# Moving eight short query-weight loads from ahead of the first key load to behind it, in a streaming decode kernel

## Chip, cores and metric

The kernel runs on one core of one Trainium2 chip. The metric is device microseconds of one execution; the time given for a kernel is the median of its runs. A difference of 0.2% (0.8 us here) is about what a measurement of this kernel can tell from no change.

## What is computed

Two branches share one input row `x` (1 x 1024) and are mixed by a gate:

```python
g = sigmoid((x * gate_w).sum(-1, keepdims=True))
# A: attention of one query row over a cache of 65536 positions, 32 query heads on 4 key/value heads of 128
q = (x @ wq).reshape(1, 1, 32, 128).transpose(0, 2, 1, 3)      # wq 1024 x 4096
scores = einsum('bhqd,bhkd->bhqk', q, repeat(k_cache, 8)) * 128 ** -0.5
a = (softmax(scores) @ repeat(v_cache, 8)).transpose(...).reshape(1, 1, 4096) @ wo   # wo 4096 x 1024
# B: gated MLP with a spatial weight of size 1 x 1
z = gelu(x @ w_in)                                             # w_in 1024 x 3584
b = (z[..., :1792] * (layernorm(z[..., 1792:]) * w_sp + b_sp)) @ w_out
out = g * a + (1 - g) * b
```

All inputs are bf16. The keys and the values are 67.1 MB each, `wq` and `wo` 8.4 MB each, `w_in` 7.3 MB, `w_out` 3.7 MB: 162 MB are read for an output of 2 KB.

## The kernel before

**A stream of large loads.** `stream` is a list of loads in a fixed order (lines 347 to 363): `wq`, the first 8 MB of keys (`load_k2(0, 0)`, called the first keys below), `w_in`, 4 MB of keys, 4 MB of keys, `w_out`, then keys and values in turns of 8 MB, at last `wo` in five parts. All are issued on SyncE's DMA queue (SP) by `issue()` at line 392, in the order of the list, into a ring in the on-chip memory with five places of 4 MB. The two keys loads of the first 8 MB take places 0 and 1, `wq` and `w_in` both take the region `VB` (places 3 and 4).

**What holds a load back.** A load may be recorded once its place's earlier user is done (`done(key)` calls `issue()` again), and then its DMA waits on SP for the engine that read the place last. So `w_in` waits for the last TensorE matmul that reads `wq` (line 507), and everything later in the list stands behind it on SP, since SP takes its instructions in order.

**The cut of `wq`.** Of the `wq` load the last 512 columns of each partition's row are left off (`w -= MC`, line 391). These 128 rows of 1 KB are fetched by `few_rows()` (line 409) with eight short DMAs, four of 20 rows into 5 x 4 pieces and four of 12 rows into 3 x 4 pieces; they land in place 2. `few_rows()` is called right behind the `wq` load, so SP's order is: `wq`, eight short loads, first keys, `w_in`, and so on.

**The query projection.** One recorded operation on TensorE (lines 494 to 511) holds 63 matmuls on the main part of `wq` (helper lines 261 and 263) and then eight on the short rows (line 507). The recorder (`Recorder.emit`) puts all of an operation's waits ahead of its first instruction, so the 63 matmuls too wait for the eight short loads. Behind it VectorE copies the result (L513), TensorE transposes it (L517), and after two more small steps (L520 to L528) GpSimd writes the padded query (`q_piece`, L536). All key work stands behind this: VectorE transposes a quarter of a keys block at a time (`k_piece`, L548, 128 x 2048 as f32), TensorE multiplies it with the query (L261, L263).

**Ahead of the start.** `R.ahead` says how many of SP's first DMAs are put ahead of the barrier with which the engines start together: 10 before, which are `wq`, the eight short loads and the first keys. `R.early` does the same for four tiny loads on ScalarE's queue.

Of the kernel before, what the change touches and what calls it, by code (L numbers as in the profile page):

```python
# [138 lines left out]
def bass_gated_mix__gqa_block_cached__mixer_gmlp__decode_kernel(  # L139
# [115 lines left out]
    R = Recorder()  # L255
# [50 lines left out]
    MC, MB = 512, 8  # L306
# [68 lines left out]
    def grains(off, w):  # L375
        return list(range(off // GRAN, (off + w + GRAN - 1) // GRAN))

    def issue():

        while issued[0] < len(stream):  # L380
            n = issued[0]
            keys, off, src = stream[n]
            w = src.shape[1]
            gr = grains(off, w)
            if any(k not in used for x in gr if x in owner for k in owner[x]):
                return
            for j, x in enumerate(gr):
                owner[x] = (keys[j * len(keys) // len(gr)],)
            cut = keys == [("wq", 0)]
            if cut:  # L390
                w -= MC
            P("SP", lambda e, o=OFF["RING"] + off, w=w, src=src[:, :w]: e.dma_start(arena[:, o:o + w], src),
              w=[("slot", x) for x in gr], dma="s%d" % gr[0])
            if cut:
                few_rows()
            issued[0] += 1

    def few_rows():

        ps = arena[:, 0:1].ap[0][0]  # L400
        at, gr, r0 = OFF["RING"] + M_AT, grains(M_AT, MC * MB), 0
        for ne, nj, j0 in FEW:
            for lo in range(4):
                a = arena[:, at:at + 1]
                a = bass.AP(tensor=a.tensor, offset=a.offset + lo * ps + MC * j0, ap=[[4 * ps, ne], [MC, nj], [1, MC]])
                b = A_wq[0:1, :]
                b = bass.AP(tensor=b.tensor, offset=b.offset + WQ_N * (KC * (r0 + nj * lo) + KC - 1) + WQ_N - MC,
                            ap=[[WQ_N * KC * 4 * nj, ne], [WQ_N * KC, nj], [1, MC]])
                P("SP", lambda e, a=a, b=b: e.dma_start(a, b), w=[("few", lo + j0)] + ([] if lo + j0 else [("slot", x) for x in gr]),  # L409
                  dma="few%d" % (lo + j0))  # L410
            r0 += 4 * ne * nj
        owner.update({x: (("wq", 0),) for x in gr})
# [6 lines left out]
    def done(key):  # L419
        used.add(key)  # L420
        issue()

    issue()


# [401 lines left out]
    P("DVE", lambda e: e.tensor_copy(orow[0:W0 + NW, :], fb[0:W0 + NW, 0:QW]), w=["orow", "fb"])  # L827
    store()

    R.ahead = 2 + MB  # L830
    R.early = 4
    R.emit(nc)

# [27 lines left out]
```

## Time and profile before

| | |
|---|---|
| time, median of 3 runs | 380.53 us (380.39 to 380.82) |
| the profiled execution: its own time, its span | 380.59 us, 379.3 us |
| bytes read from HBM | 162.01 MB, 427 GB/s over the span |
| TensorE, VectorE busy | 61%, 54% of the span |
| mean granted TensorE clock | 0.838 |
| SP issue of one short load | 0.70 to 0.93 us, 8 of them |

The span goes from the first to the last instruction of the profiled execution; 1.3 us of its time lie outside. In the profile SPq is SP's queue of DMA issues, PE is TensorE, DVE VectorE, POOL GpSimd, ACT ScalarE; L392 is line 392 of the kernel. A row of the timeline gives the start in us, the duration in us, engine, line, operation, output and input, the count, and in brackets the idle time before it and what ended it.

### The profile page before, as it was taken

The page shows a single profiled execution, that of the slowest core. Times are in us where ns is not written, and L with a number is a line of the kernel's source. Part 1 is how long each engine was busy: PE and PEld are TensorE (multiplying, and loading weights), DVE is VectorE, ACT ScalarE, POOL GpSimd, SP SyncE. Part 2 cuts the span into 40 slices and gives each one's busy share as a digit, 9 for nine tenths or more (in the row PEclk, how much of TensorE's full clock was granted, in tenths as well). Part 3 has the DMA queues.
Part 4 walks back from the last instruction along what each step waited for, and adds up shares of the span by engine and source line. Part 5 has one row for each costly group of instructions (what it writes and reads, how often), then busy time and mean ns, then how long its engine had stood idle before and what let it go on. Part 6 is the DMA issues. An engine that isn't in the chain of part 4 may idle for free.

```text
span 379.3 us, 2599 instructions
## 1 busy us (share of the span) xinstructions
PE 229.9 (61%) x1452; PEld 57.9 (15%) x844; DVE 205.6 (54%) x168; ACT 23.3 (6%) x24; POOL 9.3 (2%) x36
## 2 busy tenths in 40 slices
PE   0062289566648934895389328951995189737296
PEld 0011011011201200121012001220111011201024
DVE  1411487778479625965496249745873387412020
ACT  1000000010420000002200000022000000220000
POOL 1400000000000000000000000000000000000000
PEclk9997589798959985998599959995899589958599
DMA  9999999999999999999999999999999999999896
GB/s 436 435 415 408 433 419 422 442 456 438 408 435 442 435 444 422 422 442 435 442 437 442 429 422 429 444 442 435 429 408 430 442 435 442 437 442 435 384 432 273
DMA packets 3822, 162.17 MB, mean 428 GB/s; under 512 B 484, under 2 KB 612, under 8 KB 868
## 3 DMA queue, kind: packets, MB, share of 16 engines
q1 hardware_dynamic: 3776, 162.01, 98.9%
q8 instruction: 9, 0.15, 0.1%
q10 hardware_dynamic: 36, 0.00, 0.0%
q14 instruction: 1, 0.01, 0.0%
HBM read 162.01 MB, written 0.00 MB: 427 GB/s over the span
## 4 chain that ended last, share of the span: by engine, by line
DMA 61%; PE 17%; DVE 17%; SPq 2%; ACT 1%; issue 1%
DMA arena<-in_A_k_cache_dram 46%; DVE arena L548 16%; DMA arena<-in_A_wo_dram 8%; DMA arena<-in_A_v_cache_dram 7%; PE scp L261 7%; PE scp L263 6%; SPq L409 2%; PE obt L261 2%; PE obt L263 1%; DVE arena L585 1%; PE fbt L766 1%; ACT arena L580 1%; DVE arena L670 0%; DVE arena L668 0%; PE fbt L714 0%
## 5 line engine op out<-in xcount | busy, mean ns | idle before, releaser
L548 DVE STREAM_TRANSPOSE arena<-arena 128x2048 f32<-128x2048 f32 x64 | 143.0, 2284 | 54.9 <-DMA arena<-in_A_k_cache_dram 40.1
L261 PE MATMUL scp<-arena 128*128 128x512 bf16 (+1 forms) x274 | 111.6, 424 | 94.4 <-DVE arena L548 93.9
L263 PE MATMUL scp<-arena 128*128 128x512 bf16 (+1 forms) x275 | 110.2, 418 | 0.0
L261 PE MATMUL obt<-arena 128*64 128x512 bf16 (+2 forms) x334 | 60.7, 404 | 15.1 <-DMA arena<-in_A_v_cache_dram 14.9
L263 PE MATMUL obt<-arena 128*64 128x512 bf16 (+2 forms) x333 | 60.1, 400 | 0.0
L261 PEld LDWEIGHTS scp<-arena 128*128 128x128 bf16 (+1 forms) x274 | 27.5, 104 | 205.1 <-issue 103.9
L585 DVE STREAM_TRANSPOSE arena<-arena 128x2048 bf16<-128x2048 bf16 x7 | 16.2, 2311 | 27.0 <-PE obt L263 24.8
L580 ACT ACTIVATE arena<-arena 128x2048 bf16<-128x2048 f32 x8 | 16.0, 2002 | 217.2 <-DVE arena L577 194.1
L261 PEld LDWEIGHTS obt<-arena 128*64 128x64 bf16 (+1 forms) x334 | 17.7, 109 | 65.3 <-issue 58.5
L565 DVE TENSOR_SCALAR_CACHE_REDUCE arena<-scp 128x2048 f32<-128x2048 f32 x8 | 18.3, 2292 | 16.0 <-PE scp L263 16.0
L614 DVE RECIPROCAL arena<-mbt 128x1 f32<-128x1 f32 x4 | 0.6, 138 | 17.5 <-PE mbt L609 17.5
L588 DVE STREAM_TRANSPOSE arena<-arena 128x1024 bf16<-128x1024 bf16 x2 | 2.5, 1245 | 12.9 <-PE obt L263 12.9
L536 POOL COPY arena<-arena 32x32 bf16<-32x32 bf16 x16 | 3.3, 204 | 227.4 <-PE scp L263 207.7
L467 PE MATMUL scp<-arena 8*128 8x1 bf16 x8 | 0.7, 198 | 13.0 <-DVE arena L462 13.0
L627 PE MATMUL mbt<-arena 128*64 128x128 bf16 x8 | 1.3, 314 | 7.7 <-DVE arena L621 7.7
L766 PE MATMUL fbt<-arena 128*32 128x128 bf16 x128 | 4.2, 220 | 1.2 <-DMA arena<-in_A_wo_dram 1.2
L280 DVE MEMSET mbt<- 128x512 f32 x1 | 0.5, 485 | 7.7 <-PEq L846 7.7
L513 DVE CAST arena<-obt 97x1024 bf16<-97x1024 f32 x1 | 1.2, 1224 | 6.2 <-PE obt L507 6.2
L475 PE MATMUL mbt<-arena 1*128 1x2 bf16 x1 | 0.2, 158 | 7.2 <-DMA arena<-in_B_b_sp_dram 7.2
L827 DVE CAST arena<-fbt 36x128 bf16<-36x128 f32 x1 | 0.3, 283 | 7.3 <-PE fbt L766 7.3
L477 DVE COPY arena<-mbt 128x2 f32<-128x2 f32 x1 | 0.2, 158 | 7.3 <-PE mbt L475 7.3
L577 DVE TENSOR_REDUCE arena<-mbt 128x1 f32<-128x32 f32 x4 | 0.8, 192 | 6.0 <-PE mbt L574 6.0
(99 smaller groups left out, 62.5 us busy)
## 6 DMA issues: line engine op xcount, KB each, us to landing
arena<-in_A_k_cache_dram SPq DMA_DIRECT2D x2, 4096.0 KB, 31.7
arena<-in_A_wq_dram SPq DMA_DIRECT2D x1, 8064.0 KB, 21.7
arena<-in_B_w_in_dram SPq DMA_DIRECT2D x1, 7168.0 KB, 28.9
arena<-in_A_wo_dram SPq DMA_DIRECT2D x1, 4096.0 KB, 38.5
arena<-in_B_w_out_dram SPq DMA_DIRECT2D x1, 3584.0 KB, 20.2
arena<-in_A_wo_dram SPq DMA_DIRECT2D x1, 2048.0 KB, 27.6
arena<-in_A_wo_dram SPq DMA_DIRECT2D x1, 1280.0 KB, 30.3
arena<-in_A_wo_dram SPq DMA_DIRECT2D x1, 512.0 KB, 31.0
```

Source lines behind the costliest of these rows:

```text
L261: return e.matmul(*a, **kw)
L263: one = e.matmul(*a, **kw).ins
L409: P("SP", lambda e, a=a, b=b: e.dma_start(a, b), w=[("few", lo + j0)] + ([] if lo + j0 else [("slot", x) for x in gr]), dma="few%d" % (lo ...
L513: P("DVE", lambda e: e.tensor_copy(psb[0:97, :], ob[0:97, :]), w=["psb", "ob"])
L536: P("POOL", lambda e, pb=pb: e.tensor_copy(vw(qpad, 24 + 32 * pb, [[QP, 4], [1, 8]], 32 * pb, 32), vw(qall, 8 * g, [[32, 4], [1, 8]], 32 * ...
L548: P("DVE", lambda e: e.transpose(ktb(i).bitcast(F32), sl[:, 4096 * p:4096 * (p + 1)].bitcast(F32)), r=keys[4 * p:4 * p + 4], w=[("kt", i % ...
L565: P("DVE", lambda e: e.tensor_scalar(scs(j), scp[:, :], 0.0, None, op0=ALU.add, op1=ALU.max, accum_out=maxc[:, j:j + 1]), w=[("sc", j % 2) ...
L580: P("ACT", lambda e: e.activation(psb2, scs(j), ACTF.Exp, bias=gcol(j // 2, K_NB), scale=SCALE, accum_out=lp[:, j:j + 1]), r=[("sc", j % 2 ...
L585: P("DVE", lambda e: e.transpose(ptsb2, psb2), r=["psb"], w=[("ptsb", 0), ("ptsb", 1)])
L588: P("DVE", lambda e: e.transpose(ptsb(n), ab("PSB", 1024, 1024 * (n % 2))), r=["psb"], w=[("ptsb", n % 2)])
L627: ins = e.matmul(mb[64 * g:64 * (g + 1), 0:128], vw(sel, 128 * c, [[2, 64]]), osc[:, 128 * c:128 * (c + 1)], start=(c == 0), stop=(c == 3) ...
L766: ins = e.matmul(fb[32 * b:32 * (b + 1), 0:QW], ovz[:, z:z + 32], sl[:, o:o + QW], start=False, stop=(i == 3 and c == 7), tile_position=(0 ...
```

## The change

`few_rows()` is called behind stream entry 1, the first keys, instead of behind entry 0, `wq`; and `R.ahead` falls from 10 to 2, so that `wq` and the first keys are issued ahead of the start barrier and the eight short loads behind it. Nothing else differs.

```diff
@@ issue() @@
             P("SP", lambda e, o=OFF["RING"] + off, w=w, src=src[:, :w]: e.dma_start(arena[:, o:o + w], src),
               w=[("slot", x) for x in gr], dma="s%d" % gr[0])
-            if cut:
+            if n == 1:
                 few_rows()
             issued[0] += 1
@@ end of the kernel @@
-    R.ahead = 2 + MB
+    R.ahead = 2
     R.early = 4
     R.emit(nc)
```

SP's instructions before and after, in order (`MB` is 8):

```
before                                  after
L392 wq          128 x 32256            L392 wq          128 x 32256
L409 wq          5x4x512  x4            L392 keys        128 x 32768
L409 wq          3x4x512  x4            -- start barrier --
L392 keys        128 x 32768            L409 wq          5x4x512  x4
-- start barrier --                     L409 wq          3x4x512  x4
L392 w_in        (waits for L507)       L392 w_in        (waits for L507)
```

TensorE, VectorE, ScalarE and GpSimd have the same instructions with the same waits, in the same order, in both.

## The prediction

> **What bounds the kernel now.** I read the page's slices and DMA queues first, then the chain that ended last, then the timeline and the landing times of the first 60 us, because all that moves is there.
>
> ```profile
> DMA  9999999999999999999999999999999999999896
> q1 hardware_dynamic: 3776, 162.01, 98.9%
> HBM read 162.01 MB, written 0.00 MB: 427 GB/s over the span
> ```
>
> The bound is the load stream. SP's queue (q1) keeps 16 DMA engines busy for 98.9% of the span; by the trace's packet records at least 12 of the 16 are moving a packet at nearly every moment from 1.5 to 376 us. TensorE and VectorE are busy 61% and 54% and wait for data. So a load that comes earlier gains nothing unless the queue ran empty for it, and any time in which the queue does run empty is added to the end.
>
> The chain of waits names the instructions that the change moves:
>
> ```profile
> 5.96 0.70 SPq L409
> 6.65 0.04 issue
> 6.70 35.40 DMA arena<-in_A_k_cache_dram
> 42.12 2.32 DVE arena L548
> ```
>
> The eight L409 issues fill 0.45 to 6.65 us, the first keys are issued behind them at 6.70 and land 35.40 us later. The chain counts the issues in full (1.6% of the span), but it doesn't show that the keys stood behind `wq` in the queue for most of those 35 us: `wq` lands 21.7 us after its issue at 0.
>
> ```profile
> arena<-in_A_wq_dram SPq DMA_DIRECT2D x1, 8064.0 KB, 21.7
> arena<-in_B_w_in_dram SPq DMA_DIRECT2D x1, 7168.0 KB, 28.9
> arena<-in_A_k_cache_dram SPq DMA_DIRECT2D x7, 27.8
> ```
>
> What decides is what follows the short rows:
>
> ```profile
> 23.18 0.60 PE L261 MATMUL obt<-arena 128*1 128x512 bf16 x4 [0.18 <-DMA arena<-in_A_wq_dram]
> 28.23 1.88 PE L507 MATMUL obt<-arena 20*1 20x512 bf16 x8
> 30.14 0.34 SPq L392 DMA_DIRECT2D arena<-in_B_w_in_dram  x1
> 30.15 1.22 DVE L513 CAST arena<-obt 97x1024 bf16<-97x1024 f32 x1 [6.23 <-PE obt L507]
> 32.96 0.94 POOL L536 COPY arena<-arena 32x32 bf16<-32x32 bf16 x4 [19.17 <-DVE arena L528]
> 42.12 4.50 DVE L548 STREAM_TRANSPOSE arena<-arena 128x2048 f32<-128x2048 f32 x2 [9.22 <-DMA arena<-in_A_k_cache_dram]
> ```
>
> The projection starts when the last short load lands (23.05 us in the landing records), ends at 30.11, and 0.03 us later SP issues `w_in`. At that point the first keys still have 12 us to run (they land at 42.1). Those 12 us are the cover under which the projection is free today: 6.93 us of it plus a load's start-up fit.
>
> **SP's issues and the barrier.** Eight issues of 0.70 to 0.93 us, 6.2 us together, go from ahead of the barrier to behind it. The other engines start at about 1.3 instead of 7.54 us. Their preparation ends at 14.3 us now, and then TensorE waits until 21.5 for a tiny load that is stuck behind `wq`; 6 us earlier there is 6 us more waiting: 0. The first keys are issued at 0.45 instead of 6.70 us, but the DMA engines work on `wq` until about 21 us: 0. The eight issues now run from about 1.3 to 7.5 us, and the only instruction behind them on SP, `w_in`, is due long after: 0.
>
> **The short rows in the queue.** The landing records show one landing per DMA engine: 5 engines for four of the loads, 3 for the others. The first 1 KB packet ran at 20.8 us, just behind an engine's last `wq` packet, although SP had issued it between 0.4 and 6.7 us: on this queue an engine works in order of issue. The rows cost three engines 1.4 us and two more 0.7 us, and so the first keys land at 40.5 to 40.9 us on eleven engines and at 41.6 to 42.1 on five. After the change the same engines do `wq`, keys, rows: the same bytes, so the last short row lands where the last of the keys landed, at 42.1 us instead of 23.05 (+19). The 1.4 us of three engines are not saved, they now stand at the end of the queue.
>
> **The projection, now without cover.** TensorE starts at 42.1 + 0.13 = 42.2 us. Its 63 matmuls run side by side in groups of four, one group per 0.43 us until the clock is granted in full and one per 0.22 us from then on. Before, the full clock came 3.06 us after the first matmul: 7 groups cold, 9 warm, 5.05 us, and 1.88 us for L507: 6.93. Each further cold microsecond costs half a microsecond. In eleven places of this trace TensorE starts from rest; the clock record grants full speed 2.7 to 5.8 us after the first matmul, 4.4 on average. With 4.4 the projection takes 6.93 + 0.5 x (4.4 - 3.06) = 7.6 us; the ends are 6.75 and 8.3. I take 7.6, since in both kernels TensorE has nearly nothing to do before it. The Trainium skill, "TensorE: Matmul & The Clock Gate", Part 1, says that the clock doubles after about 3.4 us of sustained work; this trace shows 4.4 on average, and with 3.4 the sum would be 0.5 us less.
>
> **The wait that this makes.** `w_in` can be issued at 42.2 + 7.6 + 0.03 = 49.85 us instead of 30.14. Nothing else is in the queue: `w_in` stands first on SP, behind it the next two keys loads and `w_out`. From about 42 us (eleven engines: from about 40.7) until `w_in`'s packets flow, all 16 engines stand still. This is a new wait, and no work of the DMA engines hides it.
>
> **The restart.** A load with nothing ahead of it is `wq` itself: eight packets per engine of 2.38 us are 19.06 us, and its landings came at 21.05 to 21.68 us, so 2.0 to 2.6 us of start-up and receipt. The other bound is the 2 KB store at the end: issued at 378.03, landed at 379.23, 1.2 us. I take 2.0 to 2.6, the row of the same kind. The Trainium skill, "DMA: Bandwidth & Descriptors", in the section on the anatomy of one DMA, has about 2.0 us fixed for a DMA issued from GpSimd; with it the sum would be 0.3 us less.
>
> **The sum.** After the gap each engine has the same packets as before. In the landing records an engine takes 334.8 us from the landing of its first keys to that of its last `wo` piece, and 336.0 us if an instruction fetch (one 16 KB packet of about 0.95 us, on one engine at a time, eight in the run) meets it. Before, the latest engine ended at 377.2. After, all engines start alike, as if the keys had landed at 49.85 + 2.0 to 2.6 = 51.9 to 52.4, and those that meet a fetch end at 387.9 to 388.4: 10.7 to 11.2 us later, 11.0 in the middle. (51.9 to 52.4 is only 9.8 to 10.3 us past 42.1. But at the end of the run before, 13 of the 16 engines are about equally late, most of them through a fetch and not through the rows, and these move by the larger step.) Behind the last landing nothing changes.
>
> The computing moves about as far: VectorE's first L548 follows L528, which ends 2.8 us after L507, at 52.6 instead of 42.12: +10.5. The third 4 MB of keys can be issued by about 64 us, while `w_in` and the second keep the queue full to 79. In the steady part a keys load lands 27.8 us after its issue and needs 8 x 2.42 = 19.3 us plus 2 for itself: over 6 us of cover at every later issue. So no second gap.
>
> The profiled execution took 380.59 us; with 11.0 more it is 391.6. The median shown lies 0.06 lower: **391.5 us**.
>
> **Rivals.**
>
> *The short rows pass the keys* (not slower). If packets of 1 KB were served between the 64 KB ones, the rows would land by about 23 us as before, the projection would end at 30, `w_in` would follow under the keys, and as all bytes stay the same the time would be 380.5. For it: the 256-byte packets of the input row, issued at 0.12 us on ScalarE's queue, landed at 6.8 to 7.4 us in the middle of `wq`. Against it: that is another queue, and on SP's own queue the rows waited 14 us and more for `wq`. It decides if the projection starts before 35 us, where 7 us of cover are left. 0.03.
>
> *The chain is right about the issues* (faster). If the keys began to flow 6.2 us sooner, 374.3 us. The queue has no 6.2 us without packets, the slices read 9 from the first on. 0.01.
>
> *Half a gap.* If only the eight L507 matmuls waited for the rows, the other 63 would run under the keys and `w_in` would be issued after 42.2 and 1.9 to 3.5 us, near 45: the gap is 5 us shorter, 386.5. Against it: all waits of the operation stand ahead of its first matmul. 0.02.
>
> *A second gap.* If the computing fell behind the loads by more than the 6 us of cover, the surplus would come on top, 393 to 397. The likeliest place is the first two keys blocks, whose transposes start cold at 52.6; but they started cold before too (full clock 5.6 us after the first matmul, near the worst case). 0.04.
>
> **How the numbers follow.** The forecast, one gap of about 10 us, has 0.90. Its own range: projection 6.75 to 8.3 us (-0.85, +0.7), restart 1.2 to 2.7 us (-0.8 or so, +0.3), the rows' time behind the keys (+0.5 if 1 KB packets run no faster there than the slowest pair before). Both low ends give 389.8, the high ends 393.0; with a little of the second gap, 389.8 to 393.2. Faster by over 0.2%: 0.01. Within it: 0.03. Slower: 0.96.
>
> **What would show it.** In the profile after: POOL and DVE start near 1.3 us; the first L261 on `obt` starts at 42.0 to 42.5 and SP issues `w_in` at 49.1 to 50.7; the two slices of the DMA row from 38 to 57 us fall to some 3 to 6 tenths, and only these; `w_in` lands 19 to 19.6 us after its issue instead of 28.9; the steady keys loads still land about 28 us after theirs; the chain names the rows and the projection. I am wrong if the first L261 starts near 23 us, if the gap is much shorter than 9 us, or if a later slice falls too.

## The result and the profile after

The changed kernel takes 392.09 us (median of 4 runs, 391.79 to 392.85) against 380.5 us (4 runs, 380.39 to 380.82): a ratio of 1.0308, 95% interval 1.0296 to 1.032. It is slower by 11.6 us. The profiled execution took 391.79 us, with a span of 390.5 us, 11.2 us more than before.

The slices and the queues of the changed kernel. Each column of the first two lines is a fortieth of the span, 9.8 us:

```profile
DMA  9999099999999999999999999999999999999996
GB/s 423 423 430 430 13 376 411 436 431 443 431 430 430 430 431 430 430 457 430 450 445 436 430 430 436 425 436 430 430 430 431 436 443 430 438 430 430 406 428 250
q1 hardware_dynamic: 3776, 162.01, 96.3%
```

One slice, 39 to 49 us, has fallen to 0, and 13 GB/s flow in it, which are the 128 short rows. All others are as full as before. (The page counts a packet whole in the slice in which it starts. By the packets' own times this slice is busy for 0.2 and the next for 0.8 of its length.) The packets and bytes of SP's queue are the same, only its share of the span has fallen from 98.9% to 96.3%.

The same hole, in the table by stage (us of the stretch; its length; then the busy time and count of TensorE's matmuls, its weight loads, VectorE, ScalarE and GpSimd; granted TensorE clock, DMA share, GB/s):

```profile
42.00:50.50 8.50, 7.03 (x71) 1.53 (x40) 0.94 (x1) 0.00 (x0) 0.00 (x0) 1.00 0.00 0
50.50:54.00 3.50, 0.77 (x12) 0.55 (x12) 2.45 (x4) 0.00 (x0) 0.81 (x4) 0.80 1.33 508
```

For 8.5 us no packet starts, and nearly the only work is the query projection: 71 matmuls, 7.03 us (VectorE's 0.94 us is the copy behind it). Two columns need care: the 1.00 of the clock is no full speed from 42 us on, since this run's clock record begins only at 45.76 us, and a DMA share above 1 comes from packets that start in the stretch and end behind it. By the packet records the 16 engines stand still for 9.9 us more than before between 38 and 56 us, on average, and an engine's packets together take 1.0 us longer. These two make 10.9 of the 11.2 us. The timeline of the changed kernel shows how it comes about:

```profile
0.45 0.42 SPq L392 DMA_DIRECT2D arena<-in_A_k_cache_dram  x1
2.30 6.21 SPq L409 DMA_DIRECT2D arena<-in_A_wq_dram  x8
42.49 0.60 PE L261 MATMUL obt<-arena 128*1 128x512 bf16 x4 [19.49 <-DMA arena<-in_A_wq_dram]
47.64 1.88 PE L507 MATMUL obt<-arena 20*1 20x512 bf16 x8
49.55 0.34 SPq L392 DMA_DIRECT2D arena<-in_B_w_in_dram  x1
```

The short rows are issued by 8.5 us, land at 42.36 us (landing records), and TensorE starts 0.13 us later; the bracket shows 19.49 us of waiting for them where it was 0.18. `w_in` leaves SP at 49.55 us instead of 30.14. The page's list of issues, issue to landing:

```profile
arena<-in_B_w_in_dram SPq DMA_DIRECT2D x1, 7168.0 KB, 20.4
```

20.4 us instead of 28.9: the load now finds the queue empty. Shorter landing times are no good sign here. The chain of waits, which before counted the L409 issues as path, now runs from the last of them through the rows' landing and the projection to the later loads:

```profile
7.81 34.55 DMA arena<-in_A_wq_dram
42.36 0.14 issue
42.49 0.60 PE obt L261 x4
```

### The profile page after: what moved, and what is told of

Same layout as the page of the kernel before. It is cut to its first block, busy times and chain, and to the rows that moved or that the text cites. A ratio compares the mean times of both kernels' runs of the same rounds, so it can differ in the third digit from the quotient of the medians.

```text
span 390.5 us, 2599 instructions
## 1 busy us (share of the span) xinstructions
PE 231.1 (59%) x1452; PEld 58.1 (15%) x844; DVE 205.5 (53%) x168; ACT 23.3 (6%) x24; POOL 9.3 (2%) x36
## 3 DMA queue, kind: packets, MB, share of 16 engines
q1 hardware_dynamic: 3776, 162.01, 96.3%
## 4 chain that ended last, share of the span: by engine, by line
DMA 67%; PE 16%; DVE 12%; SPq 2%; ACT 1%; issue 1%
DMA arena<-in_A_k_cache_dram 43%; DVE arena L548 11%; DMA arena<-in_A_wq_dram 9%; DMA arena<-in_A_wo_dram 8%; DMA arena<-in_A_v_cache_dram 7%; PE scp L261 6%; PE scp L263 6%; PE obt L261 2%; PE obt L263 1%; SPq L409 1%; DVE arena L585 1%; PE fbt L766 1%; ACT arena L580 1%; PE obt L507 0%; PE fbt L714 0%
## 5 line engine op out<-in xcount | busy, mean ns | idle before, releaser
L261 PEld LDWEIGHTS obt<-arena 128*64 128x64 bf16 (+1 forms) x334 | 17.7, 109 | 85.1 <-issue 78.5
L766 PEld LDWEIGHTS fbt<-arena 128*32 128x32 bf16 x128 | 3.6, 97 | 2.2 <-issue 1.1
## 6 DMA issues: line engine op xcount, KB each, us to landing
arena<-in_B_w_in_dram SPq DMA_DIRECT2D x1, 7168.0 KB, 20.4
```

The source lines that it names most:

```text
L261: return e.matmul(*a, **kw)
L766: ins = e.matmul(fb[32 * b:32 * (b + 1), 0:QW], ovz[:, z:z + 32], sl[:, o:o + QW], start=False, stop=(i == 3 and c == 7), tile_position=(0 ...
```

## Experiments

The theory: one empty stretch of the load queue, because `w_in` waits for a projection that now starts when the queue is already empty. Its rivals: the start barrier and SP's issues carry part of it; the late query, and not the late `w_in`, sets the end; short rows behind 16 MB are late by their position and not by what is left to cover the projection; rows on another queue would come early.

**1. Order alone.** The changed order, but `R.ahead` as before.

```diff
-    R.ahead = 2
+    R.ahead = 2 + MB
```

> The changed order of the loads, but R.ahead left at 10, so that all ten DMAs are issued ahead of the start barrier. Theory (one empty stretch of the load queue, because the query projection now starts behind the first keys): the barrier plays no part, POOL and DVE start near 7.5 us again, w_in is issued at 49 to 50.5 us as in the changed kernel, time 391.5 to 392.9. Rival (the eight issues behind the barrier, or the barrier's earlier release, carry part of the 11 us): at least 1 us nearer to 380.5.

392.06 us (391.29 to 392.44), ratio 1.0298 (1.0281 to 1.0315). POOL's first work moves back to 7.86 us, and the time stays. The order alone makes the whole loss.

**2. Barrier alone.** The kernel before, with only `wq` ahead of the barrier.

```diff
-    R.ahead = 2 + MB
+    R.ahead = 1
```

> The order of the loads as before, but R.ahead = 1: the eight short loads and the first keys are issued behind the start barrier. Theory: the DMA engines work on wq until 21 us whatever SP does, the projection starts at 23.2 us and w_in is issued at about 30.1; 380.5, within 0.8 us. Rival (the chain of waits is right that SP's issues stand on the path): the first keys are issued about 2 us later than before (near 8.5 us) and the time moves by as much, 382 to 383.

380.48 us against 380.41, ratio 1.0 (0.9991 to 1.001). The first keys are issued at 8.36 us instead of 6.70, POOL starts at 2.12 instead of 7.54, and nothing comes of either. So the "SPq L409" share in the chain of before was no cost. In this execution the projection took 7.89 us instead of 6.93 and `w_in` was issued 1.0 us later, at 31.14: under the keys that is free as well.

**3. Only the eight matmuls wait for the rows.** On the changed kernel, the projection in two recorded operations:

```diff
+    P("PE", f, r=["xT"] + keys, w=["ob"])          # f: the 63 matmuls
+    def f(e):                                      # the eight on the short rows
...
-    P("PE", f, r=["xT", "xe"] + keys + [("few", i) for i in range(MB)] + [("slot", x) for x in grains(M_AT, MC * MB)],
+    P("PE", f, r=["xe"] + keys + [("few", i) for i in range(MB)] + [("slot", x) for x in grains(M_AT, MC * MB)],
       w=["ob"])
     done(("wq", 0))
```

> The changed kernel, with the projection recorded as two operations: the 63 matmuls on the main part wait for wq alone, the eight on the short rows wait for these; w_in still waits for the eight. Theory: the 63 run from 23.2 to 28.3 us under the keys, the eight start when the rows land (42.4 us) and, cold, take 1.9 to 3.6 us; w_in is issued at 44.4 to 46.1 us instead of 49.55 and the time falls by the same, to 386.6 to 388.5. Rival (the lateness of the query, not of w_in, sets the end: computing falls behind): the query is ready at 46 to 48 us plus 3.8 instead of 53.3, and the key work starts about as much earlier as well, so the time falls too; this run doesn't part the two, it gives the size of the empty stretch.

388.02 us (387.78 to 388.5), ratio 1.02 (1.0185 to 1.0215). The timeline of this kernel, where L511 is the eight matmuls:

```profile
42.41 3.57 PE L511 MATMUL obt<-arena 20*1 20x512 bf16 x8 [13.66 <-DMA arena<-in_A_wq_dram]
46.01 0.34 SPq L392 DMA_DIRECT2D arena<-in_B_w_in_dram  x1
```

The eight take 3.57 us from rest, 1.88 when TensorE has run before. `w_in` comes 3.54 us sooner than in the changed kernel, the profiled execution (388.14 us) 3.65 us. Of the 11.6 us of loss 7.6 stay.

**4. `w_in` released by the 63.** In addition the short rows get a key of their own, and `wq` is done after the 63.

```diff
+    done(("wq", 0))                                # after the 63
...
-    P("PE", f, r=["xe"] + keys + [("few", i) for i in range(MB)] + [("slot", x) for x in grains(M_AT, MC * MB)],
+    P("PE", f, r=["xe"] + [("few", i) for i in range(MB)] + [("slot", x) for x in grains(M_AT, MC * MB)],
       w=["ob"])
-    done(("wq", 0))
+    done(("few", 0))
@@ few_rows()
-        owner.update({x: (("wq", 0),) for x in gr})
+        owner.update({x: (("few", 0),) for x in gr})
```

> As the kernel with the projection in two operations, but w_in waits only for the 63 matmuls that read its place; the second keys load, whose place the short rows hold, waits for the eight. Theory (empty queue): w_in is issued at 28 to 29 us, under the first keys, the queue doesn't run empty though the query is ready only at about 49 to 50 us, 16 us later than before; the later loads have 6 us of cover for the 6 us by which the key work starts later: 380.5 to 381.5. Rival (late query): the key work starts at 47 to 49 us instead of 42.1 and everything behind it is late by that: 386 to 387.5.

384.58 us (384.09 to 385.61), ratio 1.0111 (1.0093 to 1.013): between the two, and I had expected neither. The timeline of SP in this kernel (a count of 2 merges two issues), and the writing of the padded query:

```profile
29.59 0.34 SPq L392 DMA_DIRECT2D arena<-in_B_w_in_dram  x1
46.09 14.03 SPq L392 DMA_DIRECT2D arena<-in_A_k_cache_dram  x2
73.69 0.33 SPq L392 DMA_DIRECT2D arena<-in_B_w_out_dram  x1
86.78 0.33 SPq L392 DMA_DIRECT2D arena<-in_A_k_cache_dram  x1
49.24 0.94 POOL L541 COPY arena<-arena 32x32 bf16<-32x32 bf16 x4 [41.85 <-DVE arena L533]
```

In the kernel before, the last two of these issues are:

```profile
67.20 0.33 SPq L392 DMA_DIRECT2D arena<-in_B_w_out_dram  x1
80.52 0.33 SPq L392 DMA_DIRECT2D arena<-in_A_k_cache_dram  x1
```

The slices of experiment 4:

```profile
DMA  9999899989989999999999999999999999999996
```

The hole at 42 us is gone, as the theory has it: by the packet records all 16 engines move packets from 38 to 44 us (the 8 there comes from counting a packet where it starts). That hole comes from `w_in`'s issue. But the query is written 16.3 us later than before (49.24 instead of 32.96), the key work behind it moves too, and the second 8 MB of keys are issued at 86.78 us instead of 80.52. The loads ahead of it land about as early as before, so the queue runs empty there, from about 85 to 87.7 us by the packet records (2.4 us on average over the engines), and once more, for 0.5 us, near 108 us. The packets of an engine together take 1.9 us longer than before. These three make 4.8 of the 5.0 us by which the profiled execution, the longest of the four (385.61 us), is slower. By the medians the late query costs 4 us of its own. The changed kernel doesn't show this cost, since its first hole delays all loads as well: by the packet records it has no hole from 80 to 125 us.

**5 and 6. A dose of cover.** The first keys as two loads with the short rows between them; c is 24576 (a quarter of the keys left as cover, 4.8 us) or 16384 (half, 9.7 us).

```diff
+            for c0, c1 in ([(0, c), (c, w)] if n == 1 else [(0, w)]):
+                gc = gr if n != 1 else grains(off + c0, c1 - c0)
-            P("SP", lambda e, o=OFF["RING"] + off, w=w, src=src[:, :w]: e.dma_start(arena[:, o:o + w], src),
-              w=[("slot", x) for x in gr], dma="s%d" % gr[0])
-            if n == 1:
-                few_rows()
+                P("SP", lambda e, o=OFF["RING"] + off + c0, w=c1 - c0, src=src[:, c0:c1]: e.dma_start(arena[:, o:o + w], src),
+                  w=[("slot", x) for x in gc], dma="s%d" % gc[0])
+                if n == 1 and c0 == 0:
+                    few_rows()
```

> The changed kernel, with the first keys issued as two loads (three quarters of each partition's row, then one quarter) and the short rows between them. A quarter of the first keys is 4.8 us of transfer. Theory: the rows land at about 37.5 us, the projection ends near 44.6, and of the 11.3 us that the change cost 4.8 are covered again: 386.6 to 387.8. Rival (behind the keys or ahead of them is what counts, not the length of work behind the rows): 391.5 or more.

387.47 us (386.8 to 388.1), ratio 1.019 (1.0173 to 1.0207).

> The same with the rows in the middle of the first keys, 9.7 us of transfer behind them. Theory: the rows land at about 32.7 us, w_in is issued at 39.5 to 40.5, 1 to 2 us ahead of the last packet of the keys; 1 to 2 us of the 11.3 are left: 381.3 to 382.8. Rival (position, not cover): 391.5 or more.

382.66 us (382.51 to 382.8), ratio 1.0058 (1.0043 to 1.0073). Each microsecond of keys left behind the rows takes back about one. Position as such doesn't set the time: both runs lie well below the 391.5 of that rival.

**7. A faster projection where nothing covers it.** The changed kernel, with matmuls on constants in TensorE's idle time ahead of it:

```diff
+    def f(e):
+        for k in range(74):
+            ins = mm(e, k > 0, tb, idb, sele, start=True, stop=True)
+        return ins
+    P("PE", f, r=["idb", KSE], w=[KTB])
```

> The changed kernel, with 74 matmuls of 512 columns on constants added on TensorE between the gate's small steps and the projection; their result is overwritten. They run from 23 to about 41 us, where TensorE has nothing to do. Theory: the projection, which nothing covers, starts at full clock and takes about 5.4 us instead of 7.0; w_in is issued 1.5 to 1.7 us earlier and the time falls by that, to 389.9 to 391.0. Rival (the added matmuls end too late, or the clock falls back in the pause before the rows land): no fall, 391.8 or more. If TensorE's time were covered, the time would stay at 391.8 to 392.9 though the projection is shorter.

389.9 us (389.8 to 390.03), ratio 1.0248 (1.0233 to 1.0264). The filling runs from 23.45 to 41.64 us, and the projection starts at full clock:

```profile
23.83 17.81 PE L263 MATMUL scp<-arena 128*128 128x512 bf16 x73
42.39 0.39 PE L261 MATMUL obt<-arena 128*1 128x512 bf16 x4 [0.75 <-DMA arena<-in_A_wq_dram]
47.86 0.34 SPq L392 DMA_DIRECT2D arena<-in_B_w_in_dram  x1
```

The projection takes 5.44 us instead of 7.03, `w_in` comes 1.69 us sooner and the profiled execution (390.03 us) 1.76 us. More work on TensorE made the kernel faster, since in this stretch the projection is the one thing on the path. The runs also lie closer together, 0.23 us from end to end where the changed kernel has 1.06.

**8. The rows on ScalarE's queue.**

```diff
-                P("SP", lambda e, a=a, b=b: e.dma_start(a, b), w=[("few", lo + j0)] + ...
+                P("ACT", lambda e, a=a, b=b: e.dma_start(a, b), w=[("few", lo + j0)] + ...
```

> The changed kernel, but the eight short loads are issued on ScalarE's DMA queue instead of SP's, behind its four tiny loads and the start barrier. Theory (within one queue a DMA engine works in order of issue, between queues in turns): the rows pass between the 64 KB packets of wq and of the keys and land well ahead of 42 us, by about 25; the projection starts at 23 to 26 us, w_in is issued under the keys, 380.5 within 0.8 us. Rival (short rows always come behind the 16 MB issued first, whatever the queue): 391.5 or more.

391.82 us (391.4 to 392.48), ratio 1.03 (1.0285 to 1.0315): not as the theory had it. The expected overtaking happens, but far too slowly. In the window from 10 to 40 us of this kernel (queue, packets, MB, share):

```profile
q1 hardware_dynamic: 208, 12.52, 96.3%
q10 hardware_dynamic: 68, 0.05, 0.5%
```

q10 is ScalarE's queue. By the packet records four of the rows' 1 KB packets started near 13.9 us, four near 16.4, four near 18.8, five near 21.1, five near 23.6, and so on about every 2.4 us (each series skips one turn between 30 and 34 us), which is the time of one 64 KB packet. The records don't name the engine, but this fits engines that take one packet from the one queue, then one from the other, however small. An engine with 32 rows to fetch then needs 32 turns. By 40.4 us, 47 of the 128 had been fetched, and the other 81 came together by 42.0 us, when SP's queue had run out.

**9. The late query by itself.** The kernel of experiment 4, with 54 matmuls on constants between the 63 and the eight:

```diff
+    P("PE", f, r=["idb", KSE], w=[KTB])            # f: 54 matmuls of 512 columns
```

> The kernel of e4_release, with 54 matmuls on constants between the 63 and the eight, so that the eight start at full clock; their result is overwritten. In e4_release the queue ran empty not at 42 but at 85 to 88 us, because the second 8 MB of keys were issued at 86.8 us instead of 80.5: behind the key work, which the late query had moved. Theory (the late query costs those 4 us): the eight take 1.9 instead of 3.6 us, the query and that keys load come 1.7 us sooner, 382.3 to 383.5. Rival (the 4 us come from the way w_in and the next loads are held back, not from the query's time): no change, 384.1 or more.

383.27 us (382.54 to 384.9), ratio 1.0087 (1.0063 to 1.011). In the profiled execution (382.54 us) the eight take 1.88 us, and the second 8 MB of keys are issued 1.57 us sooner:

```profile
85.21 0.33 SPq L392 DMA_DIRECT2D arena<-in_A_k_cache_dram  x1
```

The hole at 85 us shrinks from 2.4 to 0.9 us on average over the engines, and the one near 108 us is gone. The median falls by 1.3 us, as the theory has it, but the intervals of 4 and 9 overlap, and the two profiled executions, the longest of 4 and the shortest of 9, are 3.07 us apart. So the direction is as expected and the size is not settled.

**Taken together.** One number decides in all kernels in which `w_in` is held back: when it is issued. Profiled executions:

| kernel | `w_in` issued, us | own time, us |
|---|---|---|
| before | 30.14 | 380.59 |
| barrier alone (2) | 31.14 | 380.48 |
| rows behind half of the keys (6) | 40.46 | 382.51 |
| behind three quarters (5) | 44.90 | 386.80 |
| only the eight wait (3) | 46.01 | 388.14 |
| faster projection (7) | 47.86 | 390.03 |
| the change | 49.55 | 391.79 |
| rows on ScalarE's queue (8) | 50.37 | 392.48 |
| order alone (1) | 50.55 | 392.44 |

From 40.46 on it is a line: 10.09 us later, 9.93 us longer. Carried back to 380.5 it meets the axis near 38.5 us, some 2 us ahead of 40.3 us, where in the changed kernel the first engines end their last keys packet. By this line `w_in`'s issue is free up to there; no kernel was run in which it comes between 31.14 and 40.46 us.

No version tried beats the kernel before; that of experiment 2 equals it.

## Why the prediction was right

The forecast was 391.5 us, slower, in 389.8 to 393.2; measured 392.09. The mechanism is the one that was forecast. By its steps:

- **What bounds the kernel.** Right: the loss is time in which the load queue is empty, and the bytes and the other slices are unchanged.
- **SP's issues and the barrier at nothing.** Right, shown by experiments 1 and 2. The chain's 6.2 us, priced as the rival that would be faster, was no path. One detail was off: GpSimd starts at 2.29 us and the short rows are issued from 2.30 to 8.51, where about 1.3 to 7.5 was forecast. ScalarE issues its four tiny loads, also ahead of the barrier, until 1.77 us, which the forecast left out. Nothing hangs on that microsecond.
- **Where the rows land.** 42.1 us forecast, 42.36 measured; the first matmul at 42.49 lies in the 42.0 to 42.5 given.
- **The projection without cover.** 7.6 us forecast, 7.03 in the profiled execution. The full clock came 3.27 us after the first matmul. Over the executions seen it came after 3.06 us (projection 6.93), 3.27 (7.03), 4.10 (7.45), 4.79 (7.78), 5.01 (7.89) and 5.36 (8.07): half a microsecond per cold microsecond, as the sum had it. The Trainium skill, "TensorE: Matmul & The Clock Gate", Part 1, has about 3.4 us and says that it varies with the phase of a window; this execution agrees with the figure, the others with the variation. Uncovered, this chance is in the time: probably that is why the other runs (up to 392.85) lie above the profiled one, though only the profiled one shows its projection.
- **The restart.** 2.0 to 2.6 us beside the packets was forecast. Fourteen engines landed `w_in` at 68.3 to 68.8 us, which is 1.8 to 2.3 us; the last at 69.96, later than the forecast's 69.4 (20.4 us after the issue, where 19 to 19.6 was forecast). One instruction fetch ran in that stretch, at 59.6 us, which may be the last engine's.
- **The sum.** The last `wo` landing was forecast 10.7 to 11.2 us later, it came 11.21 later (388.44). `w_in` was issued 0.3 us earlier than forecast, and from there to the last landing it took 0.3 to 0.8 us longer. The two nearly cancelled. That the profiled execution lies within 0.2 us of its forecast (391.6 us) is in part luck.
- **No second gap.** True of the changed kernel, but for a narrower reason than given. "Over 6 us of cover at every later issue" was read from the steady keys loads and is wrong for the second 8 MB of keys: before, they are issued at 80.52 us behind `w_out`, whose last packets end from 85.1 us on, and a load needs 1.0 us from issue to its first packet (49.55 to 50.52 for `w_in` after the change), so 3.6 us of cover. Experiment 4 moved this issue by 6.3 us without moving the loads ahead of it, opened a hole of about 2.5 us there, and lost 4 in all.
- **What the profile would show.** Two slices at 3 to 6 tenths were forecast; one fell to 0 and the next reads 9. The hole is where it was forecast: eleven engines had stopped by 40.7 us, the last rows ended at 42.0, and packets flow again from 50.5. But the forecast used the slices of the shorter span (38 to 47 and 47 to 57 us). In the longer span nearly all of the hole falls into the slice from 39 to 49, and the page counts the packets after the restart whole in the next.
- **The rivals.** The rows passing the keys stayed out on SP's queue, and experiment 8 shows that even another queue lets them pass at only one packet per turn. That half a gap is left when only the eight wait was priced at 386.5; built, it gave 388.02, since the eight run from rest in 3.57 us.

## What to carry to other kernels

In a kernel that its load queue bounds, find the wait that holds the next load, and count how much transfer is still queued when that wait ends; a small transfer that such a wait depends on belongs ahead of the large load that should cover it, even if the chain of waits charges its issue to the path. When a load's time from issue to landing gets shorter, look whether the queue has run empty. After closing one hole look for the next thinnest cover: it needn't be the steady part's.

## What the hardware showed unexpectedly

Here two queues shared an engine by packets, not by bytes: in experiment 8, 1 KB packets beside 64 KB ones moved at about one per 2.4 us and engine, 47 of 128 in 27 us, where in the changed kernel the same rows behind the keys took 1.6 us (40.4 to 42.0). And the hole cost a little more than its length: the loads' packets, summed over an engine, took 1.0 us longer in the changed kernel (376.1 against 375.1 us), about half of it in the first packet of each engine after the restart, 2.66 us on average instead of 2.12.
